# An attention-and-experts kernel: exponents of the later tiles from broadcast log gates, and a new order of its first phase

## The chip, the core and the metric

The kernel runs on one core of a Trainium2 chip. The core has a matrix engine (TensorE, in the profile PE and, for its weight loads, PEld), VectorE (DVE), ScalarE (ACT), GpSimd (POOL), a sync engine (SP) that issues most transfers, and 16 DMA engines. Each engine runs its own instructions in the order in which they are written and waits on semaphores. The metric is device time in microseconds (us); lower is better.

## The reference

Three stages, all fp32:

```python
for t in range(S):                       # B=2, H=8, S=768, D=40: a gated linear recurrence
    m_new  = max(f[t] + m, i[t])
    f_stab = exp(f[t] + m - m_new); i_stab = exp(i[t] - m_new); m = m_new
    C = f_stab * C + i_stab * outer(v[t], k[t]);  n = f_stab * n + i_stab * k[t]
    y[t] = sigmoid(o[t]) * (C @ q[t]) / max(abs(n . q[t]), 1)
x = y as 1536 rows of 320
x = sum over 4 experts e of p[:, e] * (relu(x @ w1[e]) @ w2[e])     # 320 -> 1024 -> 320
out = ((x @ w_a) * (x @ w_b)) @ w_out                               # 320 -> 1536 -> 320
```

## The kernel before

The sequence is cut into 6 chunks of 128 steps; with two batches that makes 12 tiles, n = 2j + b for chunk j and batch b. Within a tile the recurrence is done as attention. `gate1` and `gate2` run two scans on VectorE: one for the running maximum m, one for the sums L of the log forget gates over the chunk. A weight between step s and step t is exp(L[t] + cm[s]), where cm is the log input gate less m and L. The kernel makes the exponent as a matrix product: `weights_of` (L447) multiplies LT, which holds ones and cm as high and low parts, by Rr, which `build_R` (L440) fills with L for the 8 heads; the product pt_a (112 rows, 512 columns) goes through one exp on ScalarE (L453) and a triangular mask on GpSimd (L454). There is one pt_a for each half of the heads of a tile, 24 in all. `scores` gives the products of keys and queries pt_c, `s1b` multiplies the two on VectorE (L470), `s2a` makes the outputs pt_y, and pt_i from the state of the chunks before; `s2b` normalises, `s3a` transposes (pt_x), and `split_hi`/`split_lo` write the high and low parts xh and xl that the experts read.

From tile 4 on, keys and queries are split too: `split_qk` (L338) casts the 120x1024 tile on ScalarE (qs_t) and subtracts twice on VectorE (L349) for the low parts.

`gate_tail` (L428) transposes the exponentiated gates (pt_e, L431) and spreads the chunk's decay to 120 rows by three small products with a constant matrix expd (L434), for which GpSimd first makes eb (L425).

Meanwhile the first three half experts run: for each pair of tiles there are 12 items, each a group psa (L208: eight 256-column products), its evictions hh on ScalarE (L275) and hl on VectorE (L276), and the second layer psy (L287 to L289) two items later. Weights come as raw fp32 pieces, are cast on ScalarE (wh, L91) and the rest is taken on VectorE or GpSimd (wl, L93), as the table LOENG says. What happens between which items is set by a hand-written list of events, `ev`, of (time in items, function, arguments); every engine's order follows from it. All transfers of this phase are issued by SP in that order, so a transfer that must wait holds those behind it. After the last pair the remaining experts and the last stage run with four-at-a-time groups (L228, L253); that part is in none of the edits.

Of the kernel before, what the change touches and what calls it, by code (L numbers as in the profile page):

```python
# [18 lines left out]
P = 128  # L19
# [17 lines left out]
QENG = ("vector", "vector")  # L37
# [11 lines left out]
def mlstm_moe_kernel(ctx, tc, gates, qk, qc, kvo, dp, w1b, w2b, ident_d, bdmask_d, rsel_d, exp_d, out):  # L49
# [256 lines left out]
    with ExitStack() as c1:  # L306
# [11 lines left out]
        expd = ac.tile([16, 3 * 120 + 2], F32, name="expd")  # L318
        rmask = ac.tile([G, P], F32, name="rmask")
        LT = [ac.tile([G, P], F32R, name=f"LT{i}") for i in range(2)]  # L320
        Rr = [ac.tile([G, H, P], F32R, name=f"Rr{b}") for b in range(B)]
        dec = ac.tile([120, NCH, 3, B], F32, name="dec")

        def load_qk(n, hh, eng=None):

            t = td.setdefault(n, {})
            if 2 <= n < NP:
                t["qk", hh] = td[n - 2]["qk", hh]
            else:
                tag, bufs = ("qs", 2) if (n, hh) == (1, 1) else ("qk", QB)  # L330
                t["qk", hh] = qp.tile([KS, 2, 512], F32, tag=tag, name="qk_t", bufs=bufs)
            v = t["qk", hh].rearrange("p a b -> p (a b)")
            if n < 2:
                (nc.gpsimd if n else nc.vector).memset(v, 0.0)
            r = D if n < NP else KS
            (eng or nc.sync).dma_start(v[0:r], qk[n, hh, 0:r])

        def split_qk(n, hh, engs=QENG):  # L338
# [32 lines left out]
        def load_gates(j):  # L371
            gt = a2.tile([G, 2, P], F32, tag="gt", name="gt")
            nc.sync.dma_start(gt, gates[:, :, j * P:(j + 1) * P])
            g_sb[j] = {"gt": gt}

        def gate1(j, eng):
            mr = a2.tile([G, P + 1], F32, tag="mr", name="mr")
            if j == 0:
                nc.gpsimd.memset(mr[:, 0:1], NEG)
            else:  # L380
                nc.scalar.copy(mr[:, 0:1], g_sb[j - 1]["mr"][:, P:])
            f, ig, m = g_sb[j]["gt"][:, 0], g_sb[j]["gt"][:, 1], mr[:, 1:]
            nc.vector.tensor_tensor_scan(m, f, ig, mr[:, 0:1] if j == 0 else g_sb[j - 1]["mr"][:, P:], op0=ALU.add, op1=ALU.max)
            cm = a2.tile([G, P], F32, tag="cm", name="cm")
            lf = a2.tile([G, P], F32, tag="lf", name="lf")
            eng.tensor_tensor(lf, f, mr[:, 0:P], op=ALU.add)
            eng.tensor_tensor(lf, lf, m, op=ALU.subtract)
            eng.tensor_tensor(cm[64:G], ig[64:G], m[64:G], op=ALU.subtract)
            g_sb[j].update(cm=cm, lf=lf, mr=mr)

        def gate2(j):
            g = g_sb[j]
            lf, cm = g["lf"], g["cm"]
# [3 lines left out]
            L = a2.tile([G, P], F32, tag="L", name="L")  # L397
            nc.vector.tensor_tensor_scan(L, rmask, lf, 0.0, op0=ALU.mult, op1=ALU.add)
            zh = a2.tile([G, P], F32R, tag="zh", name="zh")
            nc.vector.tensor_tensor(cm[64:G], cm[64:G], L[64:G], op=ALU.subtract)  # L400
            g["zh"], g["L"] = zh, L

        def gate_hi(j, copy):
            g = g_sb[j]
            copy(g["zh"][0:64], g["L"][0:64])
            copy(g["zh"][64:G], g["cm"][64:G])

        def gate3(j):
            g = g_sb[j]
            zh, L, cm = g["zh"], g["L"], g["cm"]  # L410
            zx = a2.tile([64, P], F32R, tag="zx", name="zx")
            nc.vector.scalar_tensor_tensor(LT[j % 2][64:G], zh[64:G].bitcast(F32), rsel[64:G, 16:17], cm[64:G], op0=ALU.mult, op1=ALU.add)
            nc.vector.scalar_tensor_tensor(zx, zh[0:64].bitcast(F32), rsel[0:64, 16:17], L[0:64], op0=ALU.mult, op1=ALU.add)
            g["zx"] = zx

        def gate4(j):
            g = g_sb[j]
            L, cm = g["L"], g["cm"]
            ex = a2.tile([G, P], F32, tag="ex", name="ex")
            nc.scalar.activation(ex[0:64], L[0:64], AF.Exp)  # L420
            nc.scalar.activation(ex[64:G], cm[64:G], AF.Exp, bias=L[64:G, P - 1:P])
            g["ex"] = ex
            if 0 < j < NCH - 1:
                eb = a2.tile([16, 2], F32, tag="eb", name="eb")
                nc.gpsimd.tensor_tensor(eb, expd[:, 360:362], ex[0:16, P - 1:P].to_broadcast([16, 2]), op=ALU.mult)  # L425
                g["eb"] = eb

        def gate_tail(j):  # L428
# [3 lines left out]
            if 0 < j < NCH - 1:  # L432
                for g in range(3):
                    nc.tensor.matmul(pt[0:120, 128 + 2 * g:130 + 2 * g], expd[:, g * 120:(g + 1) * 120], g_sb[j]["eb"], start=True, stop=True, skip_group_check=True)  # L434
            g_sb[j]["ET"] = ET = a2.tile([P, 96], F32, tag="ET", name="ET")
            nc.scalar.copy(ET, pt[:, 0:96])
            if 0 < j < NCH - 1:
                nc.scalar.copy(dec[:, j].rearrange("p a b -> p (a b)"), pt[0:120, 128:134])

        def build_R(n, eng, h0=0, h1=H):  # L440
            j, b = n // 2, n % 2
            zx = g_sb[j]["zx"]
            eng.tensor_tensor(
# [3 lines left out]
        def weights_of(n, hh, pool=ps_t, tag="t"):  # L447
# [4 lines left out]
            nc.tensor.matmul(pa, LT[j % 2], Rr[b][:, 4 * hh:4 * hh + 4, :].rearrange("p h t -> p (h t)"), start=True, stop=True)  # L452
            nc.scalar.activation(w, pa, AF.Exp)  # L453
# [35 lines left out]
        def s2b(n):  # L489
            j, b = n // 2, n % 2  # L490
            t = td[n]
            r = og[j][:, b].rearrange("p (h d) -> p h d", d=D)
            y = a2.tile([P, H, DE], F32, tag="y", name="y_t", bufs=1)
            pyv = t["py"][:, 0:H * DE].rearrange("p (h e) -> p h e", e=DE)
            if j > 0:
# [4 lines left out]
            else:  # L500
                y = pyv
# [21 lines left out]
        def state(n):  # L523
# [63 lines left out]
        table(AF.Exp)  # L587
        load_gates(0)
        nc.sync.dma_start(rsel, rsel_d)
        load_kvo(0)  # L590
        load_kvo(1)
        load_qk(0, 0)
        load_qk(0, 1)
        load_qk(1, 0)
        load_qk(1, 1)
        for t in LT:
            nc.vector.memset(t[0:64].bitcast(F32), 1.0)
        nc.sync.dma_start(td[0]["kvo"][:, NK:NK + NV], kvo[0, :, NK:NK + NV])
        nc.sync.dma_start(td[1]["kvo"][:, NK:NK + NV], kvo[1, :, NK:NK + NV])
# [12 lines left out]
        warm_up(WARM)
        scores(0, 0)
        scores(0, 1)
        gate1(0, V)
        for b in range(B):
            nc.scalar.copy(Rr[b][64:G], rsel[64:G, b * H:(b + 1) * H].unsqueeze(2).to_broadcast([48, H, P]))
        gate2(0)
        gate_hi(0, nc.vector.tensor_copy)
        gate3(0)  # L620
        gate4(0)
        for n in range(2):
            build_R(n, V, 0, 4)
            build_R(n, V, 4, 8)
        weights_of(0, 0, ps_b, "b")
        weights_of(0, 1, ps_b, "b")
        scores(1, 0)
        weights_of(1, 0, ps_a, "a")
        weights_of(1, 1, ps_b, "b")
        scores(1, 1)  # L630
        go(w1[:2])
        load_qk(2, 0)
        load_qk(2, 1)
        load_kvo(2)
        load_qk(3, 0)
        load_qk(3, 1)
        load_o(1, nc.sync)
        go(w0[:2])
        o_gate(0)
        for n in range(2):  # L640
            s1b(n, 0)
            s1b(n, 1)
        go(w0[:2])
        s2a(0, 0)
        s2a(0, 1)
        s2b(0)
        warm_up(1)
        s2a(1, 0)
        s2a(1, 1)
        warm_up(1)  # L650
        go(w0[2:3])
# [275 lines left out]
```

## Time and profile before

| | |
|---|---|
| time, median of 3 runs | 623.03 us (619.73 to 623.28) |
| the profiled execution's own time | 621.56 us |
| its span, first to last instruction | 619.9 us |
| PE busy | 607.9 us (98% of the span) |
| DVE, ACT, POOL busy | 421.7, 265.5, 186.5 us |
| mean granted TensorE clock | 0.994 of full speed |

Busy time of PE is the sum over records whose ends overlap the next one's start, so the cost of a product in a full stretch is read from start to start. Times in the rows are counted from the span's start. In a timeline a row is: start, duration (of xN merged instructions together), engine, line, operation, out<-in, shape, and in brackets the idle time before it and what ended that.

### The profile page before, as it was taken

The numbers are of one execution on the slowest core, as the hardware profiler recorded it, in microseconds if no ns is written. First come the engines' busy times: TensorE is split into PE (matmuls) and PEld (weight loads), VectorE is DVE, ScalarE is ACT, GpSimd is POOL, SyncE is SP. The second block draws the span as 40 slices with busy tenths as digits, with TensorE's granted clock in tenths as the row PEclk, the third lists the DMA queues.
The fourth block names the chain that finished last, engine by engine and source line by source line (L and its number), as shares of the span: only waits on it lengthen the run. The fifth ranks groups of instructions, "written<-read, shape, count | busy, mean of one in ns | idle before, by whom it ended". The sixth has DMA issues, their size and how long they took to land.

```text
span 619.9 us, 14426 instructions
## 1 busy us (share of the span) xinstructions
PE 607.9 (98%) x5850; PEld 573.3 (92%) x5851; DVE 421.7 (68%) x860; ACT 265.5 (43%) x592; POOL 186.5 (30%) x223
## 2 busy tenths in 40 slices
PE   8898999999999999999999999999999999999997
PEld 6788999999999999999999999998888888888886
DVE  8889968686754234432589989898866777874353
ACT  6667365554614333323344344354554434431221
POOL 4677352525101111234234334332232222320000
PEclk9899999999999999999999999999999999999999
DMA  7973262626202222222222222221111111200003
GB/s 218 246 219 86 68 170 57 173 65 161 61 1 57 52 54 59 71 76 79 67 73 60 70 74 67 63 64 45 49 53 41 52 38 37 61 14 2 1 25 105
DMA packets 27983, 47.04 MB, mean 76 GB/s; under 512 B 3285, under 2 KB 17869, under 8 KB 27917
## 3 DMA queue, kind: packets, MB, share of 16 engines
q1 hardware_dynamic: 15917, 26.19, 15.3%
q10 hardware_dynamic: 11520, 19.14, 11.4%
q0 software_dynamic: 480, 0.79, 0.6%
q8 instruction: 46, 0.75, 0.5%
q14 instruction: 20, 0.16, 0.1%
HBM read 43.35 MB, written 1.97 MB: 73 GB/s over the span
## 4 chain that ended last, share of the span: by engine, by line
PE 90%; DVE 4%; DMA 3%; ACT 1%; issue 1%; SPq 1%; POOL 0%; DVEq 0%; ACTq 0%; POOLq 0%
PE psy L253 27%; PE psa L228 26%; PE psb L228 11%; PE psa L208 10%; PE psy L287 3%; PE psy L289 3%; PE psy L288 3%; PE pt_y L480 2%; PE pt_c L462 1%; DMA qc_t<-in_qc 1%; DMA og_t<-in_kvo 1%; PE pt_i L486 1%; DMA kvo_t<-in_kvo 1%; DVE qs_t L349 1%; PE pt_a L452 1%; PE pt_u L530 1%
## 5 line engine op out<-in xcount | busy, mean ns | idle before, releaser
L228 PE MATMUL psa<-xh,wh 64*128 64x512 f32 x576 | 133.5, 390 | 0.0
L253 PE MATMUL psy<-wl,hh 64*128 64x320 f32 x752 | 127.2, 305 | 0.0
L253 PE MATMUL psy<-wh,hh 64*128 64x320 f32 x752 | 127.1, 305 | 0.0
L253 PE MATMUL psy<-wh,hl 64*128 64x320 f32 x752 | 127.0, 305 | 0.0
L228 PE MATMUL psa<-xh,wl 64*128 64x512 f32 x414 | 96.3, 389 | 0.0
L228 PE MATMUL psa<-xl,wh 64*128 64x512 f32 x384 | 84.6, 389 | 0.0
L228 PEld LDWEIGHTS psa<-xh,wh 64*128 64x128 f32 x576 | 79.1, 184 | 5.9 <-issue 0.9
L253 PEld LDWEIGHTS psy<-wh,hh 64*128 64x128 f32 x752 | 81.6, 184 | 0.8
L253 PEld LDWEIGHTS psy<-wl,hh 64*128 64x128 f32 x752 | 81.3, 184 | 0.8
L253 PEld LDWEIGHTS psy<-wh,hl 64*128 64x128 f32 x752 | 81.5, 184 | 0.0
L776 DVE SCALAR_TENSOR_TENSOR hl<-psa,hh 128x512 fp32r<-128x512 f32 x60 | 38.6, 685 | 55.0 <-ACT hh L775 54.7
L125 POOL TENSOR_TENSOR wl<-tp,lf 128x272 fp32r<-128x272 f32 x48 | 38.9, 811 | 114.0 <-DVE tp L124 110.3
L228 PE MATMUL psb<-xh,wh 64*128 64x512 f32 x216 | 69.7, 389 | 0.0
L228 PEld LDWEIGHTS psa<-xh,wl 64*128 64x128 f32 x414 | 59.7, 184 | 3.7
L275 ACT ACTIVATE hh<-psa 128x256 fp32r<-128x256 f32 x72 | 27.6, 383 | 75.2 <-PE psa L208 73.8
L228 PE MATMUL psb<-xh,wl 64*128 64x512 f32 x180 | 58.5, 389 | 0.0
L228 PEld LDWEIGHTS psa<-xl,wh 64*128 64x128 f32 x384 | 54.1, 184 | 3.6
L122 POOL TENSOR_TENSOR lf<-lf,sq 128x272 f32<-128x272 f32 x48 | 38.1, 794 | 61.9 <-ACT wh L121 47.9
L93 POOL TENSOR_TENSOR wl<-raw,wh 128x352 fp32r<-128x352 f32 x28 | 26.4, 946 | 94.3 <-ACT wh L91 68.7
L276 DVE SCALAR_TENSOR_TENSOR hl<-psa,hh 128x256 fp32r<-128x256 f32 x72 | 30.3, 420 | 32.7 <-ACT hh L275 32.2
L775 ACT ACTIVATE hh<-psa 128x512 fp32r<-128x512 f32 x60 | 32.6, 596 | 46.2 <-PE psy L253 26.7
L208 PE MATMUL psa<-xh,wh 128*128 128x256 f32 x216 | 51.3, 292 | 0.4 <-ACT xh L133 0.4
(141 smaller groups left out, 1451.4 us busy)
## 6 DMA issues: line engine op xcount, KB each, us to landing
raw<-in_w2b ACTq DMA_DIRECT2D x48, 272.0 KB, 2.7
qk_t<-in_qk SPq DMA_DIRECT2D x16, 480.0 KB, 7.8
raw<-in_w1b ACTq DMA_DIRECT2D x32, 176.0 KB, 2.3
acc<-in_w1b SPq DMA_DIRECT2D x24, 176.0 KB, 3.7
kvo_t<-in_kvo SPq DMA_DIRECT2D x10, 364.5 KB, 4.8
og_t<-in_kvo SPq DMA_DIRECT2D x6, 320.0 KB, 5.9
out<-acc SPq DMA_DIRECT2D x12, 160.0 KB, 1.9
qc_t<-in_qc SPq DMA_DIRECT2D x10, 180.0 KB, 2.6
```

Of the source, the lines that this page charges most:

```text
L93: lo_eng.tensor_tensor(wl[:, cs], raw, wh[:, cs].bitcast(F32), op=ALU.subtract)
L122: nc.gpsimd.tensor_tensor(lf, lf, sq, op=ALU.mult)
L125: nc.gpsimd.tensor_tensor(wl[:, cs], tf, lf, op=ALU.add)
L208: nc.tensor.matmul(ps, l, r, start=(i == 0), stop=(i == len(prs) - 1))
L228: return nc.tensor.matmul(ps[g], w[rows, o:o + P], x, start=start, stop=stop)
L253: ms = [nc.tensor.matmul(ps[t], l[rows, t * P:(t + 1) * P], w[rows, off:off + DM], start=start, stop=stop) for t, rows in zip(two, (UP, DN))]
L275: nc.scalar.activation(self.hh, ps, AF.Relu)
L276: nc.vector.scalar_tensor_tensor(self.hl, ps, 0.0, self.hh.bitcast(F32), op0=ALU.max, op1=ALU.subtract)
L287: nc.tensor.matmul(ps, lh, wh[:, off:off + DM], start=(fi == 0), stop=False)
L288: nc.tensor.matmul(ps, lh, wl[:, off:off + DM], start=False, stop=False)
L775: nc.scalar.activation(hh, ps[f], AF.Relu)
L776: nc.vector.scalar_tensor_tensor(hl, ps[f], 0.0, hh.bitcast(F32), op0=ALU.max, op1=ALU.subtract)
```

## The change

From tile 4 on (chunks j >= 2), the exponent's L part reaches all partitions by transfers: `send_L` writes the 16 rows of L to DRAM, and `spread_L` reads them back into Rr broadcast over 128 partitions (512 KB for a tile). ScalarE then computes exp of Rr with cm, transposed into ET, as a per-partition bias: one call for each head, 128 columns each. The product pt_a, `build_R`, the casts zh and the low parts LT and zx remain for tiles 0 to 3 alone. The decay is made by one transpose of the last gate column broadcast over 120 columns; expd and eb go. The first loads are issued by SP and ScalarE's queue, bring 64 rows in place of 40, and the zero fill covers the rest. LOENG moves three wl pieces of half experts 0 and 2 from GpSimd to VectorE. The order of the whole phase is a new event list.

```diff
-LOENG = {0: "ppvpvpvp", 1: "pppppppp", 2: "pppppppp", 3: "vpvpvpvp", 4: "vpvpvpvp", 5: "vpvpvpvp"}
+LOENG = {0: "ppvvvpvp", 1: "pppppppp", 2: "vpppppvp", 3: "vpvpvpvp", 4: "vpvpvpvp", 5: "vpvpvpvp"}
+JB = 2
 def load_qk(n, hh, eng=None):
-            if n < 2:
-                (nc.gpsimd if n else nc.vector).memset(v, 0.0)
-            r = D if n < NP else KS
+            r = 64 if n < 2 else D if n < NP else KS
+        def gate_c(j, eng):
+            r = slice(64 if j < JB else 0, G)
+            eng.tensor_tensor(g["cm"][r], g["cm"][r], g["L"][r], op=ALU.subtract)
+        def send_L(j, eng):
+            g_sb[j]["dL"] = dL = dr.tile([16, P], F32, tag="dL", name="dL_t")
+            eng.dma_start(dL, g_sb[j]["L"][0:16])
+        def spread_L(n, eng):
+            eng.dma_start(Rr[b].bitcast(F32).rearrange("p h t -> p (h t)"), dL[b * H:(b + 1) * H].rearrange("h t -> (h t)").partition_broadcast(P))
+        def gate5(j):
+            if j >= JB:
+                nc.scalar.copy(g["ex"][32:64], g["cm"][32:64])
             nc.scalar.activation(ex[64:G], cm[64:G], AF.Exp, bias=L[64:G, P - 1:P])
-                eb = a2.tile([16, 2], F32, tag="eb", name="eb")
-                nc.gpsimd.tensor_tensor(eb, expd[:, 360:362], ex[0:16, P - 1:P].to_broadcast([16, 2]), op=ALU.mult)
 def gate_tail(j):
             nc.tensor.transpose(pt[:, 0:96], ex[0:96, :], ident[0:96, 0:96])
-                for g in range(3):
-                    nc.tensor.matmul(pt[0:120, 128 + 2 * g:130 + 2 * g], expd[:, g * 120:(g + 1) * 120], g_sb[j]["eb"], start=True, stop=True, skip_group_check=True)
+                nc.tensor.transpose(pt[0:120, 128:224], ex[0:96, P - 1:P].to_broadcast([96, 120]), ident[0:96, 0:96])
+        def w_exp(n, hh):
+            if j < JB:
+                nc.scalar.activation(td[n]["w", hh], td[n]["pa", hh], AF.Exp)
+                return
+            for h in range(4 * hh, 4 * hh + 4):
+                nc.scalar.activation(w[:, (h % 4) * P:(h % 4 + 1) * P], Rr[b][:, h].bitcast(F32), AF.Exp, bias=g_sb[j]["ET"][:, 32 + b * H + h:33 + b * H + h])
-                (0.5, s1a, n0, 0), (1.5, s1a, n0, 1), (1.6, split_qk, n1, 0),
+                (1.5, w_exp, n0, 1), (1.5, w_mask, n0, 1), (1.6, split_qk, n1, 0), (1.6, low_qk, n1, 0, 0, V), (1.6, low_qk, n1, 0, 1, V), (2.435, s1b, n0, 0),
```

Where instructions move: TensorE around the first items of tile 4. Before:

```order
L208 MATMUL psa<-xh_72,wh_139 128x256 x2
L208 MATMUL psa<-xh_72,wl_140 128x256 x2
L208 MATMUL psa<-xl_75,wh_139 128x256 x2
L208 MATMUL psa<-xh_72,wh_139 128x256
L208 MATMUL psa<-xh_72,wl_140 128x256
L452 MATMUL pt_a<-Rr_108,LT_106 128x512
L462 MATMUL pt_c<-qs_t 128x128 x4
L287 MATMUL psy<-wh_421,hh 128x320
```

and with the change:

```order
L208 MATMUL psa<-xh_72,wh_141 128x256 x2
L208 MATMUL psa<-xh_72,wl_142 128x256 x2
L208 MATMUL psa<-xl_75,wh_141 128x256 x2
L208 MATMUL psa<-xh_72,wh_141 128x256
L208 MATMUL psa<-xh_72,wl_142 128x256
L513 MATMUL pt_c<-qs_t 128x128 x4
L287 MATMUL psy<-wh_424,hh 128x320
```

The 512-column product between the item and the scores is gone; the scores stay.

ScalarE from the copy of tile 2's x (xh, L133) to the cast of tile 3's; L574 and L633 are table loads with a one-element call, L420/L421 and L452/L458 the gates' exponents. Before:

```order
L133 CAST xh_72<-pt_x 128x3x128
L574 ACT_TABLE_LOAD
L574 ACTIVATE warm<-rmask 1x1
L275 ACTIVATE hh<-psa 128x256
L405 CAST zh<-L 64x128
L406 CAST zh<-cm 48x128
L360 ACTIVATE og_t<-og_t 128x640
L574 ACT_TABLE_LOAD
L574 ACTIVATE warm<-rmask 1x1
L275 ACTIVATE hh<-psa 128x256
L296 ACTIVATE acc<-psy,pg 128x320 x2
L420 ACTIVATE ex<-L 64x128
```

and with the change:

```order
L633 ACTIVATE warm<-rmask 1x1
L275 ACTIVATE hh<-psa 128x256
L633 ACT_TABLE_LOAD
L633 ACTIVATE warm<-rmask 1x1
L363 ACT_TABLE_LOAD
L363 ACTIVATE og_t<-og_t 128x640
L275 ACTIVATE hh<-psa 128x256
L296 ACTIVATE acc<-psy,pg 128x320 x2
L452 ACT_TABLE_LOAD
L452 ACTIVATE ex<-L 32x128
```

In this stretch there are now four table loads where there were two, and the two zh casts, which waited for VectorE, are gone. (The copy of tile 2's x and the first of the four loads stand just ahead of the rows shown.)

SP around the first loads of tiles 4 and 5 (qk_t 120x1024). Before:

```order
L357 DMA og_t<-in_kvo 128x2x320
L87 DMA acc<-in_w1b 128x352 x2
L336 DMA qk_t<-in_qk 120x1024 x3
L373 DMA gt<-in_gates 112x2x128
L367 DMA kvo_t<-in_kvo 128x729
L369 DMA qc_t<-in_qc 120x384
L336 DMA qk_t<-in_qk 120x1024
```

and with the change:

```order
L360 DMA og_t<-in_kvo 128x2x320
L334 DMA qk_t<-in_qk 120x1024
L420 DMA dL_t<-L 16x128
L426 DMA Rr_107<-dL_t 128x1024
L426 DMA Rr_108<-dL_t 128x1024
L334 DMA qk_t<-in_qk 120x1024
L376 DMA gt<-in_gates 112x2x128
L334 DMA qk_t<-in_qk 120x1024 x2
L370 DMA kvo_t<-in_kvo 128x729
```

The second to fourth key loads now stand behind the store of L and the two broadcasts.

## Rows read from the trace of the kernel before

**Rows 1.** Busy time by stretch: stretch; us; PE, PEld, DVE, ACT, POOL; PEclk; DMA
```profile
22.20:24.40 2.20, 0.25 (x2) 0.00 (x0) 2.07 (x7) 0.71 (x3) 1.08 (x2) 1.00 0.90 252
26.50:30.00 3.50, 3.50 (x19) 3.50 (x18) 1.86 (x5) 1.71 (x5) 3.50 (x4) 0.51 0.85 273
43.90:45.20 1.30, 0.30 (x4) 0.12 (x3) 1.27 (x3) 0.15 (x1) 0.24 (x1) 1.00 0.74 270
56.00:58.80 2.80, 0.26 (x4) 0.04 (x2) 2.75 (x5) 1.36 (x3) 2.72 (x5) 1.00 0.03 10
60.70:64.10 3.40, 3.08 (x13) 2.79 (x13) 3.33 (x4) 1.32 (x2) 1.73 (x1) 0.50 0.06 7
64.10:212.70 148.60, 148.60 (x1168) 147.38 (x1166) 100.27 (x225) 71.99 (x159) 44.59 (x49) 1.00 0.33 87
```

**Rows 2.** PE groups and timeline, 64 to 212 us: pt_a, and item starts
```profile
L452 PE MATMUL pt_a<-Rr,LT 112*128 112x512 f32 x16 | 6.3, 396 | 0.0
...
64.27 0.40 PE L452 MATMUL pt_a<-Rr,LT 112*128 112x512 f32 x1
64.50 0.56 PE L462 MATMUL pt_c<-qs_t 120*128 120x128 f32 x4
...
68.34 0.40 PE L208 MATMUL psa<-xh,wh 128*128 128x256 f32 x2
...
70.18 0.40 PE L208 MATMUL psa<-xh,wh 128*128 128x256 f32 x2
```

**Rows 3.** PE timeline at 93 us: gates' transpose, decay products, next item
```profile
93.06 0.25 PE L431 MATMUL pt_e<-ident,ex 96*128 96x96 f32 x1
93.23 0.79 PE L434 MATMUL pt_e<-eb,expd 16*120 16x2 f32 x6
93.95 0.39 PE L208 MATMUL psa<-xh,wh 128*128 128x256 f32 x1
```

**Rows 4.** PE timeline, 56 to 64 us: two waits
```profile
58.77 0.79 PE L434 MATMUL pt_e<-eb,expd 16*120 16x2 f32 x6 [2.54 <-POOL eb L425]
...
63.37 0.80 PE L208 MATMUL psa<-xl,wh 128*128 128x256 f32 x2 [0.32 <-DVE xl L136]
```

**Rows 5.** POOL timeline, 57 to 65 us
```profile
58.69 3.74 POOL L443 TENSOR_TENSOR Rr<-zx,rsel 64x1024 fp32r<-64x1024 f32 x2
```

**Rows 6.** DVE timeline, 57 to 64 us
```profile
57.23 5.74 DVE L349 TENSOR_TENSOR qs_t<-qk_t,qs_t 40x512 fp32r<-40x512 f32 x2
62.91 0.41 DVE L136 TENSOR_TENSOR xl<-pt_x,xh 128x256 fp32r<-128x256 f32 x1
```

**Rows 7.** DVE timeline, 101 to 107 us, first items of a pair
```profile
101.72 1.39 DVE L349 TENSOR_TENSOR qs_t<-qk_t,qs_t 40x512 fp32r<-40x512 f32 x2
...
105.71 0.67 DVE L470 TENSOR_TENSOR w_t<-pt_c,w_t 128x512 f32<-128x512 f32 x1
```

**Rows 8.** ACT timeline, 48 to 57 us
```profile
48.00 1.28 ACT L574 ACT_TABLE_LOAD   x1
49.29 0.20 ACT L574 ACTIVATE warm<-rmask 1x1 f32<-1x1 f32 x1
...
50.47 0.30 ACT L405 CAST zh<-L 64x128 fp32r<-64x128 f32 x1 [0.72 <-DVE L L398]
...
55.09 0.40 ACT L421 ACTIVATE ex<-cm,L 48x128 f32<-48x128 f32 x1
...
56.88 0.48 ACT L133 CAST xh<-pt_x 128x384 fp32r<-128x384 f32 x1
```

**Rows 9.** ACT timeline, 99 to 100 us, first items of a pair
```profile
99.56 0.39 ACT L275 ACTIVATE hh<-psa 128x256 fp32r<-128x256 f32 x1 [1.56 <-PE psa L208]
99.84 0.59 ACT L453 ACTIVATE w_t<-pt_a 128x512 f32<-128x512 f32 x1
```

**Rows 10.** PE timeline at 106 us: outputs of a tile
```profile
106.23 1.91 PE L480 MATMUL pt_y<-kvo_t,w_t 128*128 128x82 f32 x16
```

**Rows 11.** The page's list of DMA issues: KB each, us to landing
```profile
qk_t<-in_qk SPq DMA_DIRECT2D x16, 480.0 KB, 7.8
```

More of the change, by code (lines that the diff above doesn't have):

```diff
@@ L369, in load_kvo, with load_gates, gate0 @@
             nc.sync.dma_start(t["qc"], qc[n])
-        def load_gates(j):
+        def load_gates(j, eng=nc.sync):
             gt = a2.tile([G, 2, P], F32, tag="gt", name="gt")
-            nc.sync.dma_start(gt, gates[:, :, j * P:(j + 1) * P])
+            eng.dma_start(gt, gates[:, :, j * P:(j + 1) * P])
             g_sb[j] = {"gt": gt}
-        def gate1(j, eng):
-            mr = a2.tile([G, P + 1], F32, tag="mr", name="mr")
+        def gate0(j):
+            g_sb[j]["mr"] = mr = a2.tile([G, P + 1], F32, tag="mr", name="mr")
             if j == 0:
@@ new lines, in hi_L, with hi_cm, low_L, low_cm @@
+        def hi_L(j, eng):
+            g = g_sb[j]
+            copy_on(eng, g["zh"][0:64], g["L"][0:64])
+        def hi_cm(j, eng):
+            g = g_sb[j]
+            copy_on(eng, g["zh"][64:G], g["cm"][64:G])
+        def low_L(j):
+            g = g_sb[j]
+            g["zx"] = zx = a2.tile([64, P], F32R, tag="zx", name="zx")
+            nc.vector.scalar_tensor_tensor(zx, g["zh"][0:64].bitcast(F32), rsel[0:64, 16:17], g["L"][0:64], op0=ALU.mult, op1=ALU.add)
+        def low_cm(j):
+            g = g_sb[j]
+            nc.vector.scalar_tensor_tensor(LT[j % 2][64:G], g["zh"][64:G].bitcast(F32), rsel[64:G, 16:17], g["cm"][64:G], op0=ALU.mult, op1=ALU.add)
@@ L416, in gate4 @@
         def gate4(j):
             g = g_sb[j]
[L418 to L423, printed above, removed]
-                eb = a2.tile([16, 2], F32, tag="eb", name="eb")
-                nc.gpsimd.tensor_tensor(eb, expd[:, 360:362], ex[0:16, P - 1:P].to_broadcast([16, 2]), op=ALU.mult)
-                g["eb"] = eb
+            g["ex"] = ex = a2.tile([G, P], F32, tag="ex", name="ex")
@@ L428, in gate_tail @@
+            r = 64 if j < JB else 32
+            nc.scalar.activation(ex[0:r], g["L"][0:r], AF.Exp)
+        def gate5(j):
+            g = g_sb[j]
+            if j >= JB:
+                nc.scalar.copy(g["ex"][32:64], g["cm"][32:64])
+            nc.scalar.activation(g["ex"][64:G], g["cm"][64:G], AF.Exp, bias=g["L"][64:G, P - 1:P])
         def gate_tail(j):
@@ L442, in build_R @@
             zx = g_sb[j]["zx"]
+            if eng is nc.scalar:
+                for h in range(h0, h1):
+                    nc.scalar.activation(Rr[b][0:64, h], zx.bitcast(F32), AF.Copy, scale=rsel[0:64, b * H + h:b * H + h + 1])
+                return
             eng.tensor_tensor(
@@ L586, in mlstm_moe_kernel @@
         warm = ac.tile([1, 1], F32, name="warm")
[L587 to L599, printed above, removed]
@@ L613, in mlstm_moe_kernel @@
[L613 to L628, printed above, removed]
@@ L629, in mlstm_moe_kernel @@
[L629 to L651, printed above, removed]
```

252 lines of the change are left out of this document (148 added, 104 removed).

## The prediction

> **What bounds the kernel now.** I read the busy times by stretch first [rows 1]. From 64.1 to 212.7 us, where tiles 4 to 11 are worked on, TensorE is busy for the whole 148.60 us at full clock, while VectorE is busy for 100 and ScalarE for 72: there a product that goes away is worth its time from start to start, so long as no other engine comes late. Before 64.1 us TensorE waits. The stretches shown are two long idle ones (22.2 to 24.4 and 56.0 to 58.8 us), each followed some 2 us later by about 3.4 us at half clock (1.2 GHz; the column PEclk reads 0.51 and 0.50), and a shorter one (43.9 to 45.2) after which the clock held. After 212.7 us nothing is edited, and I cost it at nothing. Then I read the TensorE timeline for the prices of what goes, the three other engines around 56 to 64 us for what made TensorE wait, and ScalarE, VectorE and TensorE around 100 us for what slack the new work finds.
>
> The sum is made against the profiled execution, 621.6 us. The median of the three runs is 1.5 us above it, and they spread over 3.6, so I carry the sum over unchanged.
>
> **The change, part by part.**
>
> *Sixteen products pt_a go.* From the start of one to the start of the scores behind it is 64.50 - 64.27 = 0.23 us, and all 16 lie in the full stretch [rows 2]. 16 x 0.23 = 3.7 us gained. The work that replaces them is on ScalarE and the DMA queues, and is costed below.
>
> *The decay.* The gates' transpose and the six decay products take 93.95 - 93.06 = 0.89 us [rows 3]. The transpose alone is 0.17 from start to start; two transposes are then 0.34, so 0.55 goes for each chunk. Two such blocks stand in the full stretch (chunks 3 and 4): 1.1 us, with 0.8 to 1.5 as bounds, since a transposed broadcast column has no row here. The other two belong to the terms below.
>
> *The wait before the first pair of split tiles.* Now TensorE stands for 2.54 us at 58.77, because the decay products wait for eb, which GpSimd makes after its state updates [rows 4]. Then GpSimd fills Rr for 3.74 us [rows 5], and one of the two subtractions of tile 4's low parts lasts until that fill is over: the two take 5.74 us together [rows 6], where two take 1.39 elsewhere [rows 7]. The low part xl of tile 3 stands behind them at 62.91, so TensorE's third pair of products in item 12 starts at 63.37 [rows 4], at half clock. The change removes eb and the fill. What is late next is ScalarE. Tile 3's xh was cast from 56.88 to 57.36, behind tile 4's qs_t [rows 8]. Ahead of it the new order has two more table loads, 1.28 each [rows 8], 2.6 together, and no zh casts: each is 0.30, and the first waited 0.72 for VectorE. I take 1.4 us net, between 0.9 (both casts and their waits saved whole) and 2.6 (nothing saved). Tile 4's qs_t then ends at 56.9 + 1.4 = 58.3, two subtractions at 1.39 end at 59.7, and xl 0.41 later at 60.1. TensorE meanwhile waits about 1.2 us for the third transpose of tile 3's x, does items 11 and 12 up to xl and waits some tenths more. An idle stretch of that size at 43.9 left the clock up [rows 1], so I leave it up: what follows xl in that item takes about 0.5 us, not the 0.9 of now (63.37 to 64.27, [rows 2, 4]). Item 12 ends at 60.6 in place of 64.27: 3.6 us gained. Bounds: 5.0, if the place is reached earlier by the startup term's upper part; 1.0, if ScalarE saves nothing and both subtractions are stretched by GpSimd's state updates, which stay (5.74 us less the 3.74 of the fill is 2.0).
>
> The Trainium skill, "ScalarE: Activation LUTs", section "What ACT_TABLE_LOAD costs", speaks against this part: it puts a switch to another set at about 2.66 us, load and drain together. The two extra loads would be 5.3 us by that, this term 0.9 in place of 3.6, and the total about 617. In the trace the next call starts 1.29 us after the load does [rows 8], and I go by that.
>
> *Sixteen calls of exp become 64.* Now a call over 512 columns takes 0.59 us [rows 9]. A 128-column call with a per-partition bias is the gates' second exp: 0.40 [rows 8]. Four are 1.6; if calls overlap by 0.1, as hh and exp do now (99.84 - 99.56 against 0.39, [rows 9]), 1.3. So a group costs 0.7 to 1.0 us more. In a pair's first items ScalarE idles 1.56 us before hh at 99.56 [rows 9], which takes the first group. The second stands ahead of the cast that VectorE's subtractions at 101.72 need, and VectorE runs from there without a break to the weights of the second half, done at 106.38 [rows 7]. TensorE starts the outputs at 106.23 and needs that half 0.9 us later [rows 10]: 0.7 us of slack. The three pt_a that go ahead of it take the 0.7 away, so what ScalarE adds beyond its own idle tenths shows: 0.2 to 0.8 us for a pair. I take 0.4 for each of three pairs and 0.5 for the first, which starts with less lead: 1.7 us lost; bounds 0.4 and 3.
>
> *The transfers.* Per chunk one store of 8 KB and two broadcasts of 512 KB are added on SP's queue, ahead of three of the four key loads of that chunk. The nearest row is a 480 KB load, 7.8 us to landing at the median, with others queued [rows 11]. From chunk 3 on, the event list puts L more than 20 us before the first exp; store and broadcast, at that row's 7.8 and a few us for the small store, are 10 to 12 by my estimate, so I cost them at nothing. In chunk 2 the lead is about 10 us, and that cover is thin; it is in the bounds of the last term.
>
> *Startup.* Gates and the first keys go out on two queues, part of Rr is made on ScalarE, and one of the decay blocks and eb go at 24 us. Against that, the four first key loads bring 64 rows of 4 KB each in place of 40: 393 KB more in a stretch that moves 252 GB/s with the DMA engines at 0.90 [rows 1], 1.5 us of transfer. One more wl piece stands on VectorE ahead of the first xl. From -1.5 to +2.4 (the decay block, and the half-speed stretch at 26.5 gone), I take +0.5: the wait at 22.2 comes from a chain on VectorE whose order is kept.
>
> Moved wl pieces, the zero fill and the removed LT, zx and fills cost TensorE nothing of their own: VectorE has a third of the long stretch free [rows 1].
>
> Sum: 3.7 + 1.1 + 3.6 - 1.7 + 0.5 = 7.2. Forecast 621.6 - 7.2 = **614.4 us**.
>
> **The rivals.**
>
> *ScalarE takes over.* The extra table loads and the split exp calls hold xh, the casts and the evictions, so that the third term falls to 1 and the fourth to -3: 3.7 + 1.1 + 1 - 3 + 0.5 = 3.3, 618.3 us. For it: ScalarE is the engine that gets work at exactly the two places where slack is short. Against: it is busy less than half of the long stretch.
>
> *Both half-clock stretches and the first wait go.* The startup term at +2.4, the third at 5, the fourth at -0.8: 11.4, 610.2 us. Against: the wait at 22.2 keeps its cause.
>
> *A broadcast arrives late, and the kernel gets slower.* ScalarE runs in order; an exp that waits for Rr holds the evictions behind it, and TensorE stops two items later. To lose the 7.2 and 6.2 more, each of four pairs has to wait 3.4 us: store and broadcast would have to take about 23 us where I count 10 to 12. If they took 25, TensorE would lose some 5 us in each of three pairs and 15 in the first, 30 in all: about 644 us. For it: no row shows a broadcast read. Against: DMA engines are busy 0.33 of that stretch [rows 1].
>
> *The product does not come off the path*, since VectorE's chain to the weights has just the slack that its removal uses up: the first term halves, 616.2 us. I count this with the forecast.
>
> **How the numbers follow.** Forecast 0.66, ScalarE takes over 0.21, the upper case 0.08, the late broadcast 0.05. The terms' bounds reach from about 1 to 12 us gained; leaving out 2 in 10, I take 609 to 619.5. A measurement tells about 1% from no change: below 616.8 is faster. The forecast case gives 0.62 of its 0.66 to that, the upper case all, the second a sixth of its share: 0.74. Within 1%: 0.21. Slower by over 1%: 0.05, the late broadcast.
>
> **What would show it.** Right: in the full stretch, no pt_a, scores directly behind the item at 0.12 us, and a pair of tiles some 1 us shorter; item 12 ending near 60 us and no half clock after 57 us; the two subtractions near 1.4 us; ScalarE's four calls at 0.3 to 0.4 each. Wrong: TensorE waits in the long stretch on VectorE's weights or low parts, ScalarE waiting on DMA ahead of exp, a second half-clock stretch after 57 us, or xh of tile 3 later than 59 us.

## The result, and the profile after

The changed kernel takes 614.99 us (median of 4 runs, 614.42 to 617.0); the kernel before, run beside it, 622.19 (4 runs, 619.73 to 623.28). The ratio is 0.9895, with a 95% interval of 0.9856 to 0.9935: 7.2 us less by the medians, as forecast. The profiled execution of the changed kernel is the slowest of the four, 617.0 us with a span of 615.3; against the span of before (619.9) it shows 4.6 us gained. The account by stages is of these two executions.

The page's first part, with the busy time of each engine over the whole span:

```profile
PE 602.1 (98%) x5815; PEld 568.0 (92%) x5815; DVE 410.8 (67%) x852; ACT 278.3 (45%) x644; POOL 167.5 (27%) x208
```

Busy time by stretch of the changed kernel, in the columns of [rows 1]: the start, the place of the two waits, and the full stretch:

```profile
10.00:16.70 6.70, 6.55 (x29) 6.19 (x30) 2.81 (x6) 3.71 (x10) 2.04 (x4) 0.54 0.96 289
22.20:31.00 8.80, 6.49 (x45) 5.55 (x46) 7.79 (x23) 6.21 (x19) 2.77 (x3) 1.00 0.89 230
60.00:62.90 2.90, 2.90 (x22) 2.74 (x22) 2.40 (x6) 2.30 (x6) 0.61 (x1) 1.00 0.23 48
62.90:206.80 143.90, 143.55 (x1137) 142.82 (x1136) 96.90 (x219) 80.55 (x204) 32.13 (x41) 1.00 0.45 116
```

The stretches at half clock at 26.5 and 60.7 are gone. A new one stands at 10 to 16.7, where before had none. To see what each stage gave, one reads the same instruction in both traces. Four rows of the kernel before: the first outputs, the second state product of chunk 1 (tile 3's), and the last eviction of the full stretch.

```profile
11.30 1.91 PE L480 MATMUL pt_y<-kvo_t,w_t 128*128 128x82 f32 x16
...
53.16 0.37 PE L530 MATMUL pt_u<-kvo_t,kw_t 128*120 128x123 f32 x2
...
64.27 0.40 PE L452 MATMUL pt_a<-Rr,LT 112*128 112x512 f32 x1
...
211.90 0.38 ACT L275 ACTIVATE hh<-psa 128x256 fp32r<-128x256 f32 x1 [1.46 <-PE psa L208]
```

The same places in the changed kernel (what follows item 12 is now the scores, pt_c):

```profile
16.68 1.91 PE L527 MATMUL pt_y<-kvo_t,w_t 128*128 128x82 f32 x16
...
55.63 0.80 PE L583 MATMUL pt_u<-kvo_t,kw_t 128*120 128x123 f32 x6
...
62.91 0.56 PE L513 MATMUL pt_c<-qs_t 120*128 120x128 f32 x4
...
206.51 0.38 ACT L275 ACTIVATE hh<-psa 128x256 fp32r<-128x256 f32 x1 [1.46 <-PE psa L208]
```

So the changed kernel is 5.38 us late at the first outputs, 2.47 late at 55.6, 1.36 early at the end of item 12, and 5.39 early at the end of the full stretch. The spans differ by 4.6 only, so 0.8 is lost behind it, at the very end: the last accumulation on VectorE still starts 5.39 us early (611.07 against 616.46), but one of the last output stores takes 2.11 us to issue on SP (at 607.83) where those beside it take 0.33 to 0.41, and those behind it go out late. All ten other runs with the broadcasts have such a store (1.06 to 2.01 us); the three kernels without them (before, and runs 5 and 12 below) have none over 0.53. So it goes with the broadcasts; why is not shown.

| stage | forecast | measured (profiled executions) |
|---|---|---|
| startup, to tile 3's pt_u | +0.5 | -2.5 |
| the wait before the split tiles, to the end of item 12 | +3.6 | +3.8 |
| full stretch (16 pt_a, decay, exp calls) | +3.7 + 1.1 - 1.7 = +3.1 | +4.0 |
| behind it, in the last stores | 0 | -0.8 |
| sum | +7.2 | +4.6 |

**Why the start is late.** VectorE in the first 11 us of the changed kernel; the bracket says how long it waited and for what:

```profile
5.67 0.48 DVE L389 TENSOR_TENSOR_SCAN mr<-gt,mr 112x128 f32<-112x128 f32 x1 [2.21 <-DMA gt<-in_gates]
...
9.74 0.35 DVE L446 SCALAR_TENSOR_TENSOR LT<-zh,rsel,cm 48x128 fp32r<-48x128 f32 x1
```

and in the kernel before:

```profile
3.47 0.48 DVE L383 TENSOR_TENSOR_SCAN mr<-gt,mr 112x128 f32<-112x128 f32 x1
...
6.63 0.35 DVE L412 SCALAR_TENSOR_TENSOR LT<-zh,rsel,cm 48x128 fp32r<-48x128 f32 x1
```

The first scan of the gates starts 2.20 us later, because the gates arrive later, and LT comes 3.11 later: the other 0.9 stands between scan and LT, where the casts zh now go by ScalarE and a fill of Rr stands ahead of LT. TensorE does the first half of tile 0's scores, waits, and then works at half clock:

```profile
10.15 2.05 PE L513 MATMUL pt_c<-qk_t 120*128 120x128 f32 x8 [3.31 <-DVE LT L446]
```

The bracket names LT, which ends at 10.09, but these scores do not read it. They read the second half of tile 0's keys, whose load goes out third on ScalarE's queue, behind gates and rsel:

```profile
2.34 0.52 ACTq L334 DMA_DIRECT2D qk_t<-in_qk  x1
```

In the trace's record of semaphores the last part of that load lands at 10.02, and TensorE's wait for it is over at 10.05; in the second run of the changed kernel it is 9.58 and 9.61. So two things come late and almost together: the keys hold the scores, and LT would have held the products pt_a behind them.

**The wait before the split tiles** went as the prediction laid it out. ScalarE of the changed kernel, 49 to 61 us: four table loads (the first two at 49.61 and 51.39), the last ahead of the gates' exponents; behind them the copy that tile 3's third transpose needs, then tile 4's cast, then tile 3's xh.

```profile
52.90 1.28 ACT L363 ACT_TABLE_LOAD   x1
54.20 0.74 ACT L363 ACTIVATE og_t<-og_t 128x640 f32<-128x640 f32 x1
...
56.44 1.28 ACT L452 ACT_TABLE_LOAD   x1
...
59.19 0.24 ACT L610 COPY x_t<-x_t 128x64 f32<-128x64 f32 x1
59.34 1.05 ACT L347 CAST qs_t<-qk_t 120x1024 fp32r<-120x1024 f32 x1
60.30 0.47 ACT L133 CAST xh<-pt_x 128x384 fp32r<-128x384 f32 x1
```

VectorE behind that, and TensorE's one wait:

```profile
60.42 1.43 DVE L353 TENSOR_TENSOR qs_t<-qk_t,qs_t 40x512 fp32r<-40x512 f32 x2 [0.80 <-ACT qs_t L347]
61.78 0.41 DVE L136 TENSOR_TENSOR xl<-pt_x,xh 128x256 fp32r<-128x256 f32 x1
```

```profile
59.49 0.33 PE L147 MATMUL pt_x<-ident,x_t 128*128 128x128 f32 x1 [1.00 <-ACT x_t L610]
```

The two subtractions take 1.43 us against 5.74 [rows 6], TensorE stands for 1.00 us where 1.2 was forecast, and the clock stays up.

**The full stretch.** TensorE at 89 us, where [rows 3] had 0.89 us for transpose and decay products, and at 103 us, the outputs of a tile:

```profile
89.15 0.25 PE L463 MATMUL pt_e<-ident,ex 96*128 96x96 f32 x1
89.23 0.24 PE L465 MATMUL pt_e<-ident,ex 96*120 96x96 f32 x1
89.26 0.48 PE L208 MATMUL psa<-xh,wh 128*128 128x256 f32 x2
...
102.99 2.15 PE L527 MATMUL pt_y<-kvo_t,w_t 128*128 128x82 f32 x16
104.97 0.87 PE L533 MATMUL pt_i<-cbd_t,qc_t 120*128 120x123 f32 x6
```

Two transposes take 89.26 - 89.15 = 0.11 us, so a decay block gives 0.78, not 0.55: 1.6 for two. With 3.7 for the products 5.3 us were to be had, and 4.0 came. The rest stands in four waits. In the outputs of a pair's first tile it is 104.97 - 102.99 = 1.98 us from their start to pt_i now, and was 1.74 (106.23 to 107.97): TensorE waits 0.24 inside them, for VectorE's weights of the second half. Its weight loads (PEld) and VectorE in that pair:

```profile
104.01 0.97 PEld L527 LDWEIGHTS pt_y<-kvo_t,w_t 128*128 128x128 f32 x8 [0.16 <-DVE w_t L517]
```

```profile
99.29 1.38 DVE L353 TENSOR_TENSOR qs_t<-qk_t,qs_t 40x512 fp32r<-40x512 f32 x2 [0.23 <-ACT qs_t L347]
```

VectorE idles 0.23 for ScalarE's cast, which stands behind four exp calls, and runs without a break from there to the weights, done at 103.95. The pairs of chunks 4 and 5 have the same wait of 0.24 (134.8, 165.9). In the first pair the scores of tile 5 start 0.48 late (69.79), for low parts behind a like idle of 0.23. That makes 3 x 0.24 + 0.48 = 1.2 of the 1.3 us.

ScalarE's four exp calls of a group, and the page's line on the broadcasts (KB each, median us from issue to landing):

```profile
97.05 1.27 ACT L501 ACTIVATE w_t<-Rr,ET 128x128 f32<-128x128 f32 x4
```

```profile
Rr<-dL_t SPq DMA_DIRECT2D x8, 512.0 KB, 9.9
```

### The profile page after: what moved, and what is told of

It is laid out like the page before. It is cut to its first block, busy times and chain, and to the rows that moved or that the text cites. A ratio compares the mean times of both kernels' runs of the same rounds, so it can differ in the third digit from the quotient of the medians.

```text
span 615.3 us, 14390 instructions
## 1 busy us (share of the span) xinstructions
PE 602.1 (98%) x5815; PEld 568.0 (92%) x5815; DVE 410.8 (67%) x852; ACT 278.3 (45%) x644; POOL 167.5 (27%) x208
## 4 chain that ended last, share of the span: by engine, by line
PE 92%; DMA 3%; DVE 2%; ACT 1%; POOL 1%; SPq 1%; issue 0%; ACTq 0%; DVEq 0%
PE psy L253 27%; PE psa L228 26%; PE psb L228 11%; PE psa L208 10%; PE psy L287 3%; PE psy L289 3%; PE psy L288 3%; PE pt_y L527 3%; PE pt_c L513 1%; DMA qk_t<-in_qk 1%; PE pt_i L533 1%; DMA kvo_t<-in_kvo 1%; PE pt_u L583 1%; DMA acc<-in_w1b 1%; POOL wl L93 1%
```

## The experiments

### 1 to 4. What delayed the start

Theory "late gates": gates and rsel arrive late because key loads are now issued beside them. Rivals: the 24 additional rows of each key load, or a gain that later waits eat up. The first edit:

```diff
-(-100, load_gates, 0, nc.scalar), (-99.8, load_rsel, nc.scalar), ...
+(-100, load_gates, 0, nc.sync), (-99.8, load_rsel, nc.sync), ...
```

> The changed kernel, with the first gates and rsel issued by SP ahead of the keys instead of by ScalarE's queue beside them; the rest unchanged. Theory 'late gates' (gates landed at 5.7 and rsel at 7.2 us because 256 KB key loads share the DMA engines with them): gates land before 4.2, LT is ready near 7 instead of 10.1, TensorE's 3.3 us wait and the half clock from 10 to 16.7 go, the first outputs start near 11.5 instead of 16.7, total 611 to 612. Rival 'bytes' (64 rows in place of 40 fill the engines, whatever the order): outputs stay at 15 or later, total 614 to 616. Rival 'given back' (TensorE gets there earlier but waits for the second chunk's gates and half clock returns near 26): outputs at 11.5, total 613.5 to 615.

The second, beside it:

```diff
-(-98.5, load_qk, 0, 1, nc.scalar)
+(-98.5, load_qk, 0, 1, nc.sync)
```

> As the run with the gates first, and the one key load that ScalarE's queue issued now goes by SP too: one queue, 64 rows. 'Late gates': gates land a few tenths earlier again, near 3.5, total within 0.7 of that run (611 to 612). 'Bytes': 614 to 616.

The third, beside both (the events zero_qk go):

```diff
-            r = 64 if n < 2 else D if n < NP else KS
+            if n < 2:
+                (nc.gpsimd if n else nc.vector).memset(v, 0.0)
+            r = D if n < NP else KS
```

> As the run with one queue, and the first keys bring 40 rows after a zero fill of the whole tile, so that the first loads are as in the kernel before. 'Late gates': no further gain, within 0.7 of the one-queue run, or slower since each key load waits for its fill. 'Bytes': 2 to 4 us below the one-queue run.

The fourth is the changed kernel itself.

> The changed kernel once more, for comparison on the same chip: 614.4 to 617, first outputs between 15 and 17 us. If the start varies from run to run by 2 us, the first outputs of this profile differ from 16.7 by as much as its own time differs from 617.0.

| | us (range) | first scan starts | first outputs start | mean clock |
|---|---|---|---|---|
| changed kernel again | 615.65 (613.08 to 616.17) | 5.26 | 15.96 | 0.993 |
| gates first | 612.89 (612.78 to 613.46) | 5.29 | 13.10 | 1.000 |
| one queue, 64 rows | 611.62 (611.11 to 611.96) | 3.71 | 11.52 | 1.000 |
| one queue, 40 rows | 611.44 (610.82 to 611.64) | 3.47 | 11.29 | 1.000 |

"Late gates" is half of the answer. Putting gates and rsel first on SP did not bring the gates forward, since one key load still went out on ScalarE's queue at 0.81 us, and the gates' scan started at 5.29 all the same. With every key load behind them it starts at 3.71, the first outputs 1.6 us sooner and the total 1.3 lower. VectorE in the run with one queue:

```profile
3.71 0.48 DVE L389 TENSOR_TENSOR_SCAN mr<-gt,mr 112x128 f32<-112x128 f32 x1 [0.26 <-POOL mr L382]
...
7.45 0.35 DVE L446 SCALAR_TENSOR_TENSOR LT<-zh,rsel,cm 48x128 fp32r<-48x128 f32 x1
```

What the run with gates first gained came otherwise: the key load left on ScalarE's queue is the second half of tile 0's keys, which there lands at 4.86 in place of 10.02. The first half lands at 6.60, so TensorE waits 1.6 up to 6.7 us, does all of tile 0's scores, and then waits 0.7 for LT and 0.6 for Rr in place of 3.3, and the clock stays up. Its first outputs are 1.80 us behind the kernel before, against 5.38 in the changed kernel; LT accounts for 0.7 of the 3.6 (9.04 against 9.74). The other 2.9 are the half of the scores that no longer stands behind the wait, and the half clock; no run separates the two. "Bytes" falls: 64 rows or 40 make 0.2 us. "Given back" falls too: of 4.4 us gained at the first outputs by one queue (15.96 to 11.52), 4.0 are in the total. In that run tile 3's pt_u starts at 50.71, 2.4 us ahead of the kernel before, which is the upper end that the prediction gave the startup term. The changed kernel's runs spread over 3.1 us, these over 0.9 at most; its runs' mean clocks go with it: 0.993 or 0.994 at 616.1 to 617.0 us, 0.996 or 0.997 at 614.4 to 615.2, 1.000 at 613.08. That the half clock of the start makes the difference is likely and not shown, as only runs of 617.0 and 616.17 were profiled. Between those two the first outputs differ by 0.72 and the times by 0.83.

The next seven start from the one-queue kernel, 611.62 us. They ran on other chips than it; the kernel before took 621.6 us beside it and 621.4 and 621.3 beside them, so a few tenths between these runs are no difference.

### 5. The product back

```diff
-JB = 2
+JB = 6
-(0.5, w_exp, n0, 0), ...
+(0.5, weights_of, n0, 0), (0.5, w_exp, n0, 0), ...
-(-4.6, spread_L, n0, nc.sync), ...
+(-4.6, build_R, n0, nc.gpsimd), ...
```

> The one-queue kernel (611.6) with the exponents of tiles 4 to 11 made by the product again: 16 pt_a on TensorE, 16 exp calls of 512 columns in place of 64, Rr filled by GpSimd, no store and no broadcast; order, decay and first loads as in the one-queue kernel. Theory 'the product is worth its start-to-start time': TensorE's stretch from the first item of tile 4 on is 3.7 us longer less what the 64 calls cost it now (0.8 to 1.7), total 613.6 to 614.5; if GpSimd's fills stretch VectorE's subtractions ahead of tile 4 again (5.7 instead of 1.4 us), up to 4 more, 618. Rival 'off the path' (VectorE's chain to the weights is what ends last, with or without the product): 611.6 to 612.5.

618.15 us (618.15 to 619.29): 6.5 slower, at the upper end of what the first theory allowed. From the first eviction of the second split pair to that of the third (evictions 25 and 37) it takes 31.86 us with the product and 31.04 without, 0.82 for four products of 0.23; the next pair gives 0.92. Both are net of the 0.24 that the exp calls cost a pair in the one-queue kernel, and hold 0.1 to 0.2 of a wait at transposes. So the product is worth about its start-to-start time, and "off the path" falls. Two waits of TensorE come on top, ahead of tile 4 and at tile 5's transposes:

```profile
59.20 0.50 PE L208 MATMUL psa<-xl,wh 128*128 128x256 f32 x2 [1.52 <-DVE xl L136]
...
90.59 0.30 PE L145 MATMUL pt_x<-ident,x_t 128*128 128x128 f32 x1 [1.37 <-DVE x_t L562]
```

What made x_t late in the second I did not follow. The first is VectorE's subtractions against GpSimd's fill, each row from its engine's timeline of that run:

```profile
55.77 3.04 DVE L353 TENSOR_TENSOR qs_t<-qk_t,qs_t 40x512 fp32r<-40x512 f32 x2 [0.79 <-ACT qs_t L347]
```

```profile
55.92 4.66 POOL L482 TENSOR_TENSOR Rr<-zx,rsel 64x1024 fp32r<-64x1024 f32 x2
```

One by one, the second subtraction starts at 56.53 and ends at 58.81, and the first fill ends at 58.27: the subtraction is over 0.54 us after the fill lets go.

### 6. One exp call in place of four

```diff
-            for h in range(4 * hh, 4 * hh + 4):
-                nc.scalar.activation(w[:, ...128 columns], Rr[b][:, h], AF.Exp, bias=...h)
+            nc.scalar.activation(w, Rr[b][:, 4 * hh:4 * hh + 4], AF.Exp, bias=...4 * hh)
```

> The one-queue kernel with one exp call of 512 columns for each group of four heads, all four with the bias column of the first head (so the exponents of the other three heads are wrong): 16 calls in place of 64. Prediction's term for the calls: 1.7 us lost, so 609.9. If the trace of the changed kernel is read rightly (3.7 + 1.1 gained and only 4.0 seen from 62.9 us on), 0.8, so 610.8. Rival 'hidden': 611.6.

The one call takes the first head's bias; those of the other three are left out. 612.78 us (612.32 to 613.1): no gain, 1.2 slower. A group falls from 1.27 to 0.71 us. In the last pair that gives back what the calls had cost: the outputs run through, and by the evictions the pair is 0.23 us shorter than in the one-queue kernel.

```profile
161.66 1.91 PE L526 MATMUL pt_y<-kvo_t,w_t 128*128 128x82 f32 x16
```

In the pairs before, where VectorE also makes the next chunk's gates, the mask on GpSimd now starts earlier, into that arithmetic:

```profile
61.61 0.64 POOL L504 TENSOR_SCALAR_AFFINE_SELECT w_t<-w_t 128x512 f32<-128x512 f32 x1 [1.64 <-ACT w_t L500]
```

```profile
61.62 0.77 DVE L396 TENSOR_TENSOR lf<-lf,mr 112x128 f32<-112x128 f32 x1
62.31 1.00 DVE L298 SCALAR_TENSOR_TENSOR acc<-psy,pg,acc 128x320 f32<-128x320 f32 x2
```

That subtraction takes 0.29 us in the one-queue run, and the accumulation behind it starts at 61.73; TensorE then waits 0.21 for it. In chunks 3 and 4 it comes again, and the wait in the outputs grows from 0.24 to 0.43. All three terms on record (1.7, 0.8, 0) expected no loss.

### 7 and 8. The transfers

```diff
-            eng.dma_start(Rr[b]..., dL[b * H:(b + 1) * H]...partition_broadcast(P))
+            for _ in range(2):
+              eng.dma_start(Rr[b]..., dL[b * H:(b + 1) * H]...partition_broadcast(P))
```

> The one-queue kernel with each of the eight broadcasts of 512 KB issued twice, one after the other. Theory 'covered': 611.6 within 0.5, ScalarE never waits for Rr from chunk 3 on; in chunk 2, where the lead is thin, up to 2 us. Rival 'late broadcast': the second one ends after the first exp in all four chunks, 5 us or more lost.

630.73 us (626.05 to 631.79): 19 us lost. It looks like the late broadcast, and is not: the second copy into the same tile waits on SP for the first, and the key loads stand behind it. SP's waits (us in total, times, longest) and ScalarE in the first pair:

```profile
SPq L427 <- DMA Rr<-dL_t: 4.3, 1, 4.3
```

```profile
62.86 1.04 ACT L347 CAST qs_t<-qk_t 120x1024 fp32r<-120x1024 f32 x1 [6.29 <-DMA qk_t<-in_qk]
...
64.09 1.26 ACT L502 ACTIVATE w_t<-Rr,ET 128x128 f32<-128x128 f32 x4
```

ScalarE waits for tile 4's keys; its exp calls behind do not wait for Rr. So the traffic was doubled again without the wait, the second copy into a spare tile in DRAM:

```diff
+            spare = dr.tile([P, H * P], F32, tag="spare", name="spare", bufs=8)
+            for d in (Rr[b]..., spare):
+                eng.dma_start(d, dL[b * H:(b + 1) * H]...partition_broadcast(P))
```

> The one-queue kernel with each of the eight broadcasts followed by a second one of the same 512 KB into spare DRAM, for which nothing waits: the traffic doubled without a wait on SP. If the 19 us that the doubled broadcasts cost were SP held behind the first one's landing (key loads stood behind it): chunks 3 to 5 lose nothing, chunk 2 some 2 to 4 us (1 MB more ahead of a key load for which ScalarE waits already 0.4 us): 612 to 616. If they were the bytes: 3 us or more in every chunk, 624 or more.

613.26 us (612.61 to 613.54). All of it is in chunk 2, where the key load is behind 1 MB more; from chunk 3 on ScalarE waits for no transfer, and the evictions keep one distance of 2.0 us:

```profile
59.19 1.05 ACT L347 CAST qs_t<-qk_t 120x1024 fp32r<-120x1024 f32 x1 [2.62 <-DMA qk_t<-in_qk]
```

### 9 and 10. The waits that are left

```diff
-(8.793, o_gate, 2)
+(8.5, o_gate, 2)
```

> The one-queue kernel with the sigmoid of chunk 2 moved between its two table loads, so that two of the four table loads there go (2.6 us of ScalarE). Theory 'ScalarE's loads hold the copy of tile 3's x': TensorE's wait of 1.2 us for the third transpose at 53.2 goes, total 610.4. Rival 'given back': the wait moves to the low part xl or to the low parts of tile 4, total 611.2 to 611.8. If a switch cost 2.66 as the loads' page has it, 5 us of ScalarE would go and the wait at 53.2 with it, the same total.

611.47 us (611.0 to 611.68): no difference. The wait for the third transpose is gone, and xl is late in its place, because the subtractions now lie beside GpSimd's state updates (2.46 in place of 1.43):

```profile
54.18 2.46 DVE L353 TENSOR_TENSOR qs_t<-qk_t,qs_t 40x512 fp32r<-40x512 f32 x2 [0.79 <-ACT qs_t L347]
```

```profile
57.03 0.50 PE L208 MATMUL psa<-xl,wh 128*128 128x256 f32 x2 [0.81 <-DVE xl L136]
```

Then xh and xl were put ahead of tile 4's cast, and L of chunk 1 ahead of its cm:

```diff
-(10.9, x_hi, 3), (10.9, x_lo, 3), (10.117, split_qk, 4, 0), ...
+(10.62, x_hi, 3), (10.63, x_lo, 3), (10.64, split_qk, 4, 0), ...
-(1.45, gate2, 1), (1.45, gate_c, 1, V), (0.4, gate_i, 1, V)
+(0.41, gate2, 1), (0.42, gate_i, 1, V), (0.43, gate_c, 1, V)
```

> The one-queue kernel with three moves: the sigmoid of chunk 2 between its two table loads (as in the run before), tile 3's xh and xl ahead of tile 4's first cast and low parts, and chunk 1's second scan (L) ahead of its cm, of a wl piece and of hl on VectorE. Theory: the wait of 1.2 us near 53 goes and does not come back at xl, because VectorE no longer has the two stretched subtractions in front of it; the wait of 1.9 us for pt_e near 24.9 falls to about 0.9, since L is ready 1.2 us earlier: total 609.4. Rival 'given back': the waits move to hl of item 3, to tile 4's first scores or to the later ones, total 611 to 611.8.

611.08 us (610.82 to 611.2): half a microsecond by the medians (0.5 also against run 11, which ran beside it), the fastest of all, below both kernels; its interval against the kernel before is 0.9808 to 0.9861. By the evictions 1.1 us are gained from tile 4 on, not 2.2: L is there 1.05 us earlier (its scan starts at 22.65, not 23.70), but LT behind it is later (25.80, not 24.99), and tile 4's scores wait 0.45 for their low parts.

### 11. The moved wl pieces

LOENG's rows 0 and 2 as before.

> The one-queue kernel with the wl pieces on the engines of the kernel before (LOENG's old rows 0 and 2: three more pieces on GpSimd, three fewer on VectorE). The prediction costs the move at nothing: 611.6 within 0.5. Rival: GpSimd's three pieces of about 1 us come late for the first items or stretch VectorE's work beside them, 1 us or more lost.

611.59 us (611.3 to 611.77). The move costs nothing, as said.

### 12. GpSimd's fill, in the kernel before

```diff
-(10.0, build_R, 4, nc.gpsimd), ... (11.0, build_R, 5, nc.gpsimd)
+(10.0, build_R, 4, V), ... (11.0, build_R, 5, V)
```

> The kernel before, with Rr of tiles 4 and 5 filled by VectorE instead of GpSimd. If GpSimd's fill of 3.7 us is what stretched the two subtractions to 5.7 us: they take about 1.4 again, less than 2.5, and even with some 2.6 us of fill on VectorE ahead of them xl comes 1.5 us or so earlier than 62.91, total 619 to 620.5 against 621.4. If it was something else (the state updates, or the subtractions themselves): they still take over 4 us and xl comes 2 us later, total 623 to 624.

623.5 us (622.01 to 623.6), ratio 1.0025 (1.0008 to 1.0042). The forecast time fell and its mechanism held. The subtractions take 1.71, not 5.74, and xl comes at 60.14, not 62.91. But VectorE's fill now holds GpSimd's state update, eb comes later, and TensorE stands 3.41 us for it in place of 2.54 [rows 4]:

```profile
56.78 1.36 DVE L443 TENSOR_TENSOR Rr<-zx,rsel 64x1024 fp32r<-64x1024 f32 x1
...
58.50 1.71 DVE L349 TENSOR_TENSOR qs_t<-qk_t,qs_t 40x512 fp32r<-40x512 f32 x2
60.14 0.41 DVE L136 TENSOR_TENSOR xl<-pt_x,xh 128x256 fp32r<-128x256 f32 x1
```

```profile
57.14 1.82 POOL L536 TENSOR_TENSOR cbd_t<-cbd_t 120x369 f32<-120x369 f32 x1
58.93 0.63 POOL L425 TENSOR_TENSOR eb<-expd,ex 16x2 f32<-16x2 f32 x1
```

So moving the fill alone gave nothing; the change took the fill and eb away together.

## Why the prediction was right, step by step

- **The sum** is right by the medians, and partly by luck: one of its terms is wrong. In the profiled executions the wait came out 0.2 and the full stretch 0.9 better than forecast, the startup 3.0 worse, and 0.8 went in the last stores, where nothing was costed: 4.6 in place of 7.2. The medians give 7.2 because the other runs of the changed kernel are 2.0 to 2.6 us shorter than its profiled one, and the median before is 0.6 above its own.
- **Sixteen products**: right. 0.82 and 0.92 us for four in a pair, by the product put back and net of the exp calls' 0.24, against 0.93 forecast.
- **The decay**: mechanism right, size small. 0.78 for a block, not 0.55; the transposed broadcast column adds next to nothing, and 1.6 for two lies just above the bound of 1.5.
- **The wait before the split tiles**: right, 3.8 against 3.6. The third transpose waited 1.0 (1.2 forecast), the subtractions took 1.43 (1.39), the clock held. xl came at 61.78, not 60.1, for the start was late; tile 3's xh at 60.30 is past the 59 us that the prediction named as a sign of being wrong, for the same reason. Row and rule: the subtraction that meets the fill ends half a microsecond after it. The Trainium skill, "SBUF — State Buffer", section "Who interferes with whom", says that a VectorE instruction with two inputs in SBUF contends with a GpSimd instruction that reads SBUF, and calls the port pair that they share an exclusive lock; the rows agree (in run 5 the subtraction ends 0.54 us after the fill, in run 6 one of 0.29 us takes 0.77 beside the mask, in run 12 GpSimd's add takes 1.82 beside VectorE's fill). On the table loads the trace decided against the Trainium skill's 2.66 us for a switch ("ScalarE: Activation LUTs", section "What ACT_TABLE_LOAD costs"): the sigmoid starts 1.30 after its load (52.90 to 54.20).
- **Exp calls**: mechanism right, size somewhat less. A group is 1.27 us, within the forecast of 1.3 to 1.6, and the calls hold the cast, VectorE's chain and the outputs as laid out. It is 0.24 for each of three pairs, not 0.4, and at most 0.48 in the first, where 0.5 was taken: 1.2 against 1.7. Run 6 gives the 0.23 back in the last pair, and loses more in the others to the mask. TensorE's wait for VectorE's weights, named as a sign of being wrong, is there, but small.
- **The transfers**: right. From chunk 3 on even twice the traffic hides; chunk 2 has the thin cover, 2.0 us lost there for twice the traffic. The late broadcast has a relative that the prediction missed: not ScalarE's wait for Rr, but SP's wait in front of the key loads. And the slow store at the end, some 0.8 us, goes with the broadcasts.
- **Startup**: this step failed. "From -1.5 to +2.4, I take +0.5" priced the queues by bytes (1.5 us of transfer) and gave no load a later arrival, though gates, rsel and keys now go out side by side. The bytes made 0.2. In their place the arrivals did it: the second half of tile 0's keys, third on ScalarE's queue, landed at 10.02, the gates' scan started 2.2 us late and LT came 3.1 late, and TensorE stood for 3.31 us and lost the clock behind it, 5.4 us at the first outputs. 2.9 of the 5.4 came back by 55.6 us; the half clock at 26.5 and the wait at 43.9 are gone. The term measured -2.5, outside its own bounds; with the old order of the first loads it is +2.4.
- **The rivals**: "ScalarE takes over" (618.3) and "the product does not come off the path" (616.2) did not happen. "Both half-clock stretches and the first wait go", 610.2, is where the kernel goes when the start is mended (611.1 to 611.6); the first wait itself stays, at 1.6 us in the one-queue run, and no clock is lost by it.

## What to carry to other kernels

The loads that the first work waits for go out alone and first: a second queue does not carry large loads beside them for nothing, even if the bytes are the same. Price a reorder by the arrival of each transfer that something waits for, and add the half clock that a longer wait brought here. Where a row's bracket names an engine, ask whether the instruction reads what that engine wrote; if not, look for the load that landed just before. When two engines block each other, moving one holder to the other may only turn the hold round, as in run 12.

## What the runs showed of the hardware

- A small load is late beside large ones on another queue: the gates' scan starts at 3.71 when all key loads are issued behind gates and rsel, and at 5.26 to 5.67 when one or more are issued beside them. A key load of 256 KB issued at 2.34 behind two others on ScalarE's queue lands at 10.02; issued alone there at 0.81, at 4.86. What in the DMA engines holds them is not shown.
- TensorE's wait of 3.31 us up to 10.15 was followed by a mean clock of 0.54 from 10 to 16.7; the waits of 1.6, 0.7 and 0.6 in its place, and 1.6 at 24.9 in the one-queue run, by full clock.
- A 512 KB broadcast from 4 KB of DRAM lands in 9.9 us at the median among other loads; the same bytes once more behind each cost 2.0 us, all in chunk 2, when no instruction on the queue waited, and 19 us over four chunks when one did.
- ScalarE's 128-column exp with a per-partition bias takes 0.40 us and starts 0.29 behind the one before it in a row (97.05, 97.35, 97.64, 97.93).
